# The last gather of each expert cut from 128 rows to 32, and its transpositions with it

## The chip, the cores and the metric

The kernel runs on one core of a Trainium2 chip. The metric is the device time of one execution in microseconds, the median of several runs. The engines are TensorE (PE, with its weight loads listed apart as PEld), VectorE (DVE), ScalarE (ACT), GpSimd (POOL) and SyncE (SP); sixteen DMA engines move data between HBM and SBUF.

## The reference, cut to what matters

A causal attention with a decaying bias gives 2304 rows of 512 features (`x`). A router then deals the rows out to eight experts, 288 rows each, and every expert runs two matrix products on its own rows. A dense two-layer network follows.

```python
N, D, E, F = (2304, 512, 8, 1024)
cap = N // E                      # 288 rows for each expert
logits = x @ w_gate
order = np.argsort(-logits.flatten())
# greedy: a row goes to the best expert that still has room
for e in range(E):
    mask = assigned == e
    h = np.maximum(x[mask] @ w1[e], 0.0)
    out[mask] = h @ w2[e]
# then, on all 2304 rows
h = np.maximum(x @ w_in, 0.0)
return h * h @ w_out
```

## The kernel before, in words

The attention stage writes its 2304 rows to a DRAM tensor `xd`. The routing (`route_phases`) finds one expert after the other; for the expert of number `e` it leaves a tile `idxs[e]` of 128 x 3 row numbers. Column 0 holds the rows in places 0 to 127 of that expert, column 1 those in places 128 to 255, and column 2 those in places 256 to 287; the other 96 entries of column 2 are 0.

`gather(e, c)` (line 1090) has POOL issue one indirect DMA for column `c`: 128 rows of 2 KB of `xd` land in `XG[:, c, :]`, one row in each partition. Three gathers make up an expert. `XG` is one buffer, so an expert's gathers start only when the transpositions of the expert before have read it.

The first expert product wants the features in the partitions. `xt(e, d)` (line 1095) makes the `d`-th block of 128 features: three transpositions on TensorE (line 1102), one for each `c`, go side by side into one PSUM tile `p`, with `XG[:, c, 128d:128d+128]` as the weights and the identity `cn.ident` as the moving operand. ACT and DVE then read `p[:, :CAP]`, that is 288 columns, and split them into a high and a low part (lines 1106 and 1107). The last 96 of the 384 columns that the transpositions write are not read. For expert 0 `xt0(c)` (line 1109) does the transpositions by `c` first, four feature blocks in a row (line 1113), as soon as that gather has landed; between them stand routing steps and warming products (line 1389).

The order of blocks (`order`) is written out by hand: products with `w1` (kind 1), with `w2` (kind 2), and the dense network in chunks of experts (kinds 3 and 4). `need(e)` queues the gathers and the `xt` steps of an expert, and the main loop pops them between blocks at due times. So on TensorE the three transpositions of an `xt` stand between matrix products, mostly alone, sometimes two `xt` in a row. POOL's queue holds the gathers, the indirect stores of result rows (line 1299) and some subtractions.

Lines 308 and 311 (attention, probabilities by values) and line 338 (transpositions of attention rows) are not touched by the change, but their rows are used below. Line 308 has weights of 64 columns and writes 64 PSUM partitions; line 338 has a form with weights of 64 columns, too.

Of the kernel before, what the change touches and what calls it, by code (L numbers as in the profile page):

```python
# [34 lines left out]
def f32(ap):  # L35
    return ap.bitcast(FT)
# [496 lines left out]
CAP = 288  # L533
# [480 lines left out]
def experts(tc, cn, L, xd, w1, w2, win, wout, out):  # L1014
    nc = tc.nc
    V, S, G, T = nc.vector, nc.scalar, nc.gpsimd, nc.tensor
# [53 lines left out]
    eids, idxs = [], []  # L1070
# [16 lines left out]
    XG = fx.tile([128, 3, DM], FT, name="rows")  # L1087
    XT, P0 = {}, []

    def gather(e, c):  # L1090

        G.indirect_dma_start(out=XG[:, c, :], out_offset=None, in_=xd,
                             in_offset=bass.IndirectOffsetOnAxis(ap=idxs[e][:, c:c + 1], axis=0))

    def xt(e, d, spare=False):
        if d == 0:
            XT[e] = (wk.tile([128, 4, CAP], FR, name="xH", bufs=1), wk.tile([128, 4, CAP], FR, name="xL", bufs=1))
        if e:
            p = ps.tile([128, 512], FT, name="h", bufs=2) if spare and cn.held and d % 2 else rps.tile(
                [128, 512], FT, name="mi")  # L1100
            for c in range(3):
                T.transpose(p[:, 128 * c:128 * c + 128], XG[:, c, 128 * d:128 * d + 128], cn.ident)  # L1102
        else:
            p = P0[d]
        hi, lo = XT[e]
        S.activation(hi[:, d, :], p[:, :CAP], AF.Copy)
        V.tensor_tensor(lo[:, d, :], p[:, :CAP], f32(hi[:, d, :]), op=OP.subtract)

    def xt0(c):
        for k in range(4):  # L1110
            if c == 0:
                P0.append(ps.tile([128, 512], FT, name=f"acc{k}"))
            T.transpose(P0[k][:, 128 * c:128 * c + 128], XG[:, c, 128 * k:128 * k + 128], cn.ident)

    RAWS, W = {}, {}

# [234 lines left out]
    def need(e):  # L1351
        if lw[0] is None:
            xrows(99)
            late_stores(nc, cn, 0)
            cn.otp.__exit__(None, None, None)
            lw[0] = pool("m_lw", 2, side="right")
        while len(idxs) <= e:

            route_step()
        if e not in gathered:  # L1360
            gathered.add(e)
            if e and [e - 1, e] in CHUNKS:

                for c in range(3):
                    gather(e, c)
                soon.extend((xt, (e, d, True), 0) for d in range(4))
                return
            for c in range(3):
                if e >= GE:
                    gathers.append((e, c, at[0] + GD + GS * c))  # L1370
                else:
                    gather(e, c)
            for d in range(4):
                side.append((xt, (e, d), at[0] + (GD + 2 * GS if e >= GE else 0) + SD))

    def side_step():
        f, a, _ = side.popleft()
        while f is xt and gathers:
            gather(*gathers.popleft()[:2])
        f(*a)  # L1380
# [14 lines left out]
    for c in range(3):  # L1395
        for _ in range(RF[2 * c]):
            route_step()
        xt0(c)
        if c < 2:
            warm(WU[c + 1])  # L1400
        for _ in range(RF[2 * c + 1]):
            route_step()
# [14 lines left out]
    for n, blk in enumerate(order):  # L1417
# [10 lines left out]
        if blk[0] == 1:  # L1428
            while any(a[0] == blk[1] for f, a, _ in soon):
                xt(*soon.popleft()[1])  # L1430
            while any(f is xt and a[0] == blk[1] for f, a, _ in side):
                side_step()
# [16 lines left out]
        k, e, f = blk  # L1449
        if k > 2:  # L1450
            e = CHUNKS[e][-1]
# [67 lines left out]
```

## Time and profile before

| | |
|---|---|
| median of 3 runs | 907.24 us (907.17 to 908.33) |
| the profiled execution | 909.57 us, of which the span from the first to the last instruction is 907.7 us |
| TensorE busy | 865.0 us, 95% of the span |
| VectorE, ScalarE, GpSimd busy | 62%, 51%, 31% |
| moved by DMA | 96.10 MB |
| mean granted TensorE clock | 0.977 of full speed |

A matrix product's row gives its start and a modelled duration that includes its way through the array, so products that follow each other overlap in the rows; what a product costs the engine is read from start to start. `PE` and `PEld` rows of one instruction belong together: the load of the weights, then the product. A number in square brackets is idle time of the engine ahead of the instruction, with what ended it.

### The profile page before, as it was taken

The numbers are of one execution on the slowest core, as the hardware profiler recorded it, in microseconds if no ns is written. First come the engines' busy times: TensorE is split into PE (matmuls) and PEld (weight loads), VectorE is DVE, ScalarE is ACT, GpSimd is POOL, SyncE is SP. The second block draws the span as 40 slices with busy tenths as digits, with TensorE's granted clock in tenths as the row PEclk, the third lists the DMA queues.
The fourth block names the chain that finished last, engine by engine and source line by source line (L and its number), as shares of the span: only waits on it lengthen the run. The fifth ranks groups of instructions, "written<-read, shape, count | busy, mean of one in ns | idle before, by whom it ended". The sixth has DMA issues, their size and how long they took to land.

```text
span 907.7 us, 17252 instructions
## 1 busy us (share of the span) xinstructions
PE 865.0 (95%) x6168; PEld 735.7 (81%) x6168; DVE 564.0 (62%) x1557; ACT 463.1 (51%) x1061; POOL 278.2 (31%) x259
## 2 busy tenths in 40 slices
PE   5899999998799899999999999999999999999996
PEld 4677777777599787889997888999788999898885
DVE  7687878877786779747757457677433353432222
ACT  7687778776235666534533233454333454543332
POOL 2555555530113355524001000201000534513323
PEclk9999999997799899999999999999999999999999
DMA  6787887834555623106522001752000440230001
GB/s 158 192 203 197 224 235 192 216 93 135 174 145 148 196 82 105 59 2 209 152 59 70 1 1 38 215 152 62 24 1 1 142 126 1 82 94 0 1 1 47
DMA packets 77285, 96.10 MB, mean 106 GB/s; under 512 B 10480, under 2 KB 55536, under 8 KB 77200
## 3 DMA queue, kind: packets, MB, share of 16 engines
q1 hardware_dynamic: 71184, 79.64, 31.6%
q0 software_dynamic: 3360, 11.01, 3.7%
q10 hardware_dynamic: 2656, 4.36, 1.5%
q8 instruction: 48, 0.79, 0.4%
q14 instruction: 37, 0.30, 0.1%
HBM read 80.83 MB, written 9.44 MB: 99 GB/s over the span
## 4 chain that ended last, share of the span: by engine, by line
PE 70%; DVE 5%; DMA 3%; issue 2%; ACT 1%; POOL 1%; SPq 0%; DVEq 0%; POOLq 0%; ACTq 0%
PE h L1135 11%; PE h L1136 11%; PE h L1137 11%; PE acc L1183 7%; PE acc L1184 7%; PE acc L1185 7%; PE acc L1135 4%; PE acc L1137 3%; PE acc L1136 3%; PE mi L744 2%; DMA raw<-in_w 1%; PE mi L1102 1%; PE acc L44 1%; DVE junk L244 1%; PE pt L278 1%
## 5 line engine op out<-in xcount | busy, mean ns | idle before, releaser
L1245 ACT ACTIVATE s<-h 128x512 f32<-128x512 f32 (+1 forms) x80 | 44.4, 556 | 200.1 <-PE h L1137 173.7
L1249 DVE TENSOR_TENSOR s<-s 128x512 f32<-128x512 f32 (+1 forms) x80 | 51.1, 639 | 140.7 <-ACT sH L1248 140.6
L1135 PE MATMUL h<-yH,winH 128*128 128x512 f32 (+1 forms) x332 | 123.3, 371 | 0.0
L1136 PE MATMUL h<-yL,winH 128*128 128x512 f32 (+1 forms) x332 | 120.9, 364 | 0.0
L1137 PE MATMUL h<-yH,winL 128*128 128x512 f32 (+1 forms) x332 | 120.7, 363 | 0.0
L1183 PE MATMUL acc<-wH,sH 128*128 128x512 f32 x288 | 114.8, 399 | 0.0
L1059 ACT ACTIVATE wH<-raw 128x512 fp32r<-128x512 f32 x128 | 79.8, 628 | 67.0 <-DMA raw<-in_w 41.5
L1185 PE MATMUL acc<-wH,sL 128*128 128x512 f32 x288 | 112.5, 390 | 0.0
L1184 PE MATMUL acc<-wL,sH 128*128 128x512 f32 x288 | 112.4, 390 | 0.0
L1250 POOL TENSOR_TENSOR sL<-s,sH 128x512 fp32r<-128x512 f32 (+1 forms) x48 | 68.1, 1418 | 131.0 <-DVE s L1249 131.0
L1062 DVE TENSOR_TENSOR wL<-raw,wH 128x512 fp32r<-128x512 f32 x104 | 74.4, 718 | 46.7 <-ACT wH L1059 44.4
L256 ACT ACTIVATE e<-sc,nm 128x576 f32<-128x576 f32 (+2 forms) x144 | 80.2, 557 | 36.7 <-DVE junk L244 34.2
L244 DVE TENSOR_SCALAR_CACHE_REDUCE junk<-sc 128x576 bf16<-128x576 f32 (+2 forms) x144 | 75.6, 525 | 35.4 <-PE sc L224 26.1
L1135 PE MATMUL h<-xH,wH 128*128 128x288 f32 x256 | 79.2, 309 | 2.5 <-DVE hL L1213 1.9
L1135 PE MATMUL acc<-hH,wH 128*128 128x288 f32 x256 | 78.3, 306 | 1.7 <-ACT wH L1059 1.7
L1137 PE MATMUL h<-xH,wL 128*128 128x288 f32 x256 | 76.7, 300 | 0.8 <-POOL wL L1062 0.8
L1136 PE MATMUL h<-xL,wH 128*128 128x288 f32 x256 | 77.0, 301 | 0.1
L1137 PE MATMUL acc<-hH,wL 128*128 128x288 f32 x256 | 76.2, 298 | 0.3 <-DVE wL L1062 0.3
L1136 PE MATMUL acc<-hL,wH 128*128 128x288 f32 x256 | 76.0, 297 | 0.0
L1137 PEld LDWEIGHTS h<-yH,winL 128*128 128x128 f32 x332 | 62.7, 189 | 10.7
L1135 PEld LDWEIGHTS h<-yH,winH 128*128 128x128 f32 x332 | 62.8, 189 | 10.1
L1136 PEld LDWEIGHTS h<-yL,winH 128*128 128x128 f32 x332 | 62.9, 189 | 9.6
(236 smaller groups left out, 2028.2 us busy)
## 6 DMA issues: line engine op xcount, KB each, us to landing
raw<-in_w SPq DMA_DIRECT2D x128, 256.0 KB
k<-in_kT SPq DMA_DIRECT2D x30, 288.0 KB
q<-in_qT SPq DMA_DIRECT2D x30, 288.0 KB
r<-in_wout SPq DMA_DIRECT2D x16, 512.0 KB
r<-in_win SPq DMA_DIRECT2D x15, 512.0 KB
vb<-in_vm SPq DMA_DIRECT2D x16, 256.0 KB
Q<-Q SPq DMA_DIRECT2D x16, 144.0 KB
QB<-Q SPq DMA_DIRECT2D x14, 144.0 KB
```

What stands on the lines that cost most here:

```text
L244: nc.vector.tensor_scalar(o, v, -0.125, None, op0=OP.mult, op1=OP.min, accum_out=nm[:m])
L256: nc.scalar.activation(o, v, AF.Exp, bias=nm[:m], scale=0.125, accum_out=sums[b % 2][:m, i, hd % H:hd % H + 1] if i else both[b % 2][:, p: ...
L1059: S.activation(hi, src, AF.Copy)
L1062: (G if eng[1] == "G" else V).tensor_tensor(lo, src, f32(hi), op=OP.subtract)
L1135: T.matmul(o, wh, xh, start=first, stop=False)
L1136: T.matmul(o, wh, xl, start=False, stop=False)
L1137: T.matmul(o, wl, xh, start=False, stop=last)
L1183: T.matmul(o, hi[:, c0:c0 + 128], wh, start=f == 0, stop=False)
L1184: T.matmul(o, hi[:, c0:c0 + 128], wl, start=False, stop=False)
L1185: T.matmul(o, lo[:, c0:c0 + 128], wh, start=False, stop=f == NB2 - 1)
L1249: V.tensor_tensor(s, s, s, op=OP.mult)
L1250: (V if CHUNKS[c][0] in QUIET else G).tensor_tensor(lo, s, f32(hi), op=OP.subtract)
```

## The change

The gather of column `c` fetches `m = min(128, CAP - 128 * c)` rows, so 128, 128 and 32. The transpositions use the first `m` partitions of `XG`, the upper left `m` x `m` corner of the identity, and write `m` columns. Their weights are then 32 rows by 128 columns for `c = 2`, the moving operand 32 x 32.

```diff
     def gather(e, c):
 
-        G.indirect_dma_start(out=XG[:, c, :], out_offset=None, in_=xd,
-                             in_offset=bass.IndirectOffsetOnAxis(ap=idxs[e][:, c:c + 1], axis=0))
+        m = min(128, CAP - 128 * c)
+        G.indirect_dma_start(out=XG[:m, c, :], out_offset=None, in_=xd,
+                             in_offset=bass.IndirectOffsetOnAxis(ap=idxs[e][:m, c:c + 1], axis=0))
+
+    def flip(p, c, d):
+        m = min(128, CAP - 128 * c)
+        T.transpose(p[:, 128 * c:128 * c + m], XG[:m, c, 128 * d:128 * d + 128], cn.ident[:m, :m])
 
     def xt(e, d, spare=False):
...
             for c in range(3):
-                T.transpose(p[:, 128 * c:128 * c + 128], XG[:, c, 128 * d:128 * d + 128], cn.ident)
+                flip(p, c, d)
...
-            T.transpose(P0[k][:, 128 * c:128 * c + 128], XG[:, c, 128 * k:128 * k + 128], cn.ident)
+            flip(P0[k], c, k)
```

## Rows read from the trace of the kernel before

**Rows 1.** The page, part 4: shares of the chain that ended last, by engine.
```profile
PE 70%; DVE 5%; DMA 3%; issue 2%; ACT 1%; POOL 1%; SPq 0%; DVEq 0%; POOLq 0%; ACTq 0%
```

**Rows 2.** Windows: length, then busy time (and instructions) by engine, clock, DMA share, GB/s.
```profile
core 0: us, PE busy (x) PEld busy (x) DVE busy (x) ACT busy (x) POOL busy (x), PEclk, DMA share, GB/s
230.00:245.00 15.00, 12.77 (x102) 8.57 (x103) 11.57 (x42) 3.85 (x9) 3.15 (x3) 0.73 0.60 188
...
317.00:900.00 583.00, 580.95 (x3753) 506.73 (x3751) 318.12 (x740) 252.05 (x474) 146.65 (x140) 1.00 0.22 66
```

**Rows 3.** The tile `rows` (XG): count, duration min/median/max in ns, first and last start, shape.
```profile
L1102 PE MATMUL mi<-ident,rows x78: 270/272/308, 271.8 to 743.7; 128*128 128x128 f32 x78
L1092 POOL DMA_INDIRECT rows<-xd,idx x24: 945/987/1455, 232.5 to 729.2; - x24
...
L1113 PE MATMUL acc<-ident,rows x12: 272/273/328, 236.2 to 240.6; 128*128 128x128 f32 x12
...
L1102 PE MATMUL h<-ident,rows x6: 272/272/273, 589.1 to 591.6; 128*128 128x128 f32 x6
...
DMA to landing us min/median/max: 3.3/4.0/5.7
```

**Rows 4.** Timeline of PE, then of PEld, at the first `xt` pair of expert 1.
```profile
271.81 0.81 PE L1102 MATMUL mi<-ident,rows 128*128 128x128 f32 x6
272.38 0.38 PE L1135 MATMUL acc<-hH,wH 128*128 128x288 f32 x1
272.60 0.29 PE L1136 MATMUL acc<-hL,wH 128*128 128x288 f32 x1
...
272.36 0.19 PEld L1135 LDWEIGHTS acc<-hH,wH 128*128 128x128 f32 x1
```

**Rows 5.** Timeline of PE at the last `xt` of expert 7.
```profile
743.47 0.49 PE L1102 MATMUL mi<-ident,rows 128*128 128x128 f32 x3
743.71 0.36 PE L1135 MATMUL h<-yH,winH 128*128 128x256 f32 x1
```

**Rows 6.** Timeline of PE in the attention: transpositions with weights of 64 columns.
```profile
99.39 0.60 PE L338 MATMUL pt<-ident,oT 128*64 128x128 f32 x4
99.82 0.27 PE L278 MATMUL pt<-ident,e 128*128 128x128 f32 x1
```

**Rows 7.** Timeline of PE and PEld around products that write 64 partitions (L308).
```profile
200.87 0.27 PE L282 MATMUL pt<-ident,e 128*128 128x128 f32 x1
...
201.07 0.19 PEld L308 LDWEIGHTS av<-eT,vb 128*64 128x64 f32 x3 [0.17 <-issue]
...
201.28 0.45 PE L308 MATMUL av<-eT,vb 128*64 128x192 f32 x6
201.66 0.44 PE L278 MATMUL pt<-ident,e 128*128 128x128 f32 x2
```

**Rows 8.** Groups of PE by shape: busy us, mean ns, idle before.
```profile
L308 PE MATMUL av<-eT,vb 128*64 128x320 f32 x180 | 27.5, 441 | 0.0
...
L308 PE MATMUL av<-eT,vb 128*64 128x64 f32 x60 | 4.3, 220 | 0.0
```

**Rows 9.** Groups of PEld by shape, with 128 and with 68 rows of weights.
```profile
L221 PEld LDWEIGHTS sc<-K,Q 128*128 128x128 f32 x160 | 32.0, 200 | 10.9 <-DVE Q L173 8.3 <-ACT e L256 2.1
...
L222 PEld LDWEIGHTS sc<-K,Q 68*128 68x128 f32 x80 | 15.3, 191 | 0.0
```

**Rows 10.** Timeline of PE (last row PEld) at expert 0's second and third transpositions.
```profile
238.82 0.66 PE L1113 MATMUL acc<-ident,rows 128*128 128x128 f32 x4 [0.24 <-DMA rows<-xd,idx]
239.31 0.38 PE L1389 MATMUL h<-onesb 128*128 128x512 bf16 x1
239.53 0.65 PE L744 MATMUL mi<-oh,wide 128*128 128x8 bf16 x20
240.21 0.65 PE L1113 MATMUL acc<-ident,rows 128*128 128x128 f32 x4
241.04 0.40 PE L1135 MATMUL h<-xH,wH 128*128 128x288 f32 x1 [0.17 <-ACT xH L1106]
...
239.50 0.58 PEld L744 LDWEIGHTS <-wide 128*128 128x128 bf16 x20 [0.20 <-DVE wide L640]
```

## The prediction

> **What bounds the kernel now.** I read the chain of work that ended last first, then busy time by stretch, then the touched tile, then TensorE's timeline around it. The chain is 70% TensorE, and GpSimd has 1% of it, DMA 3% [rows 1]. The stretches show why: from 317 to 900 us TensorE is busy 580.95 of 583.00 us at full clock, while GpSimd has 146.65 us of work there and the DMA engines are used to 22% [rows 2]. Whatever lengthens or shortens the engine's stream there moves the end by the same amount; GpSimd and DMA time there is free. Only the short stretch where expert 0 starts (230 to 245 us) is not of this kind: clock 0.73, TensorE idle at times, waits on gathers.
>
> The tile view of the gathered rows gives the counts [rows 3]: 24 gathers; 78 + 6 transpositions of line 1102, so 84, of which every third one, 28, is a third-column transposition of experts 1 to 7; and 12 of line 1113, of which 4 are expert 0's. So 8 gathers and 32 transpositions change. In the timeline the 84 stand in 22 runs: six runs of two `xt` (the first is in [rows 4]) and sixteen of one (the last is in [rows 5]). Hence 6 of the 28 are followed by another transposition, and 22 by a matrix product.
>
> **The gathers.** One costs GpSimd about 1 us (median 987 ns) and lands 3.3 to 5.7 us after its issue [rows 3]. A third gather with a quarter of the rows may cost GpSimd anything between the same and a quarter, so 0 to 0.75 us each, 6 us in all, and moves 192 KB less. All of this lies beside TensorE's stream. The rows of line 1102 show no wait for a gather: TensorE goes from a product into them without a gap [rows 4, 5]. For expert 0 the second gather is waited for (0.24 us), but it is issued ahead of the third and is not changed. The third column's transpositions start at 240.21, right behind the 20 small products of line 744, which began at 239.53 and wait on routing, not on rows [rows 10]. An earlier landing of the third gather therefore opens nothing. I take 0 us; if it did speed up expert 0 after all, the whole stay at 240.21 could only move up to the end of those products, so less than 0.05 us.
>
> **What a transposition costs now.** Six of them start at 271.81 and the load behind them at 272.36, so with the first one's load ahead they go at about 0.11 us apiece [rows 4]; the four with weights of 64 columns go at (99.82 - 99.39) / 4 = 0.11 us, too [rows 6]. Half the weights, same pace: the moving operand of 128 columns sets it, not the load. A column of fp32 moves in (441 - 220) / (320 - 64) = 0.86 ns [rows 8], so 128 take 0.11 us and 32 take 0.03 us.
>
> What follows a transposition limits the saving. The load of a product of line 1135 starts at 272.36; the product is recorded 0.02 us later but lasts 0.38 us against 0.29 us, so it is held up by 0.09 us and truly starts 0.11 us after its load [rows 4]. That load can start only with the last transposition, so with a 32-column transposition ahead the wait of 0.11 us stays: nothing saved in 22 of 28 cases. With another transposition behind it the load takes about 0.06 us: in [rows 7] the two of line 278 take 0.44 us against 0.27 + 0.11 = 0.38 us, because their first load had no cover. So 0.05 us are saved in 6 cases, 0.3 us, and about 0.2 us at expert 0's four. If nothing else happened, the sum would be -0.5 us.
>
> **What 32 rows may do to the array.** The trace has no product with 64 rows or fewer, so its cost is bounded from the nearest rows. Line 308 has weights of 64 columns and asks for no place in the array. Around it TensorE stands still: the transposition of line 282 starts at 200.87 and would be done with its columns after 0.11 us, but the next load starts at 201.07, with idle time marked ahead of it [rows 7]; that is 0.09 us. On the way back the last product of line 308 starts at 201.28 + 0.45 - 0.22 = 201.51 (64 columns, 220 ns, [rows 8]), its columns take 0.055 us, and the next load starts at 201.66: 0.095 us. In both directions the first load is not covered, another 0.06 us, or 0.11 us for the load of a product. So a change between the full array and a part of it empties the array, and costs 0.15 to 0.20 us.
>
> Does a 32-row transposition count as a part? For it: line 308 gets its part by its size alone. Against it: the transpositions with 64 weight columns in [rows 6] follow and precede full ones with no gap at all, and the loads with 68 rows [rows 9] belong to the full array. The Trainium skill (TensorEngine Tiling (Array Packing), Key Properties) states that changing the tiling mode drains TensorE; the gaps of [rows 7] agree with it. The same page (Restrictions) takes column tiling, but not row tiling, away from fp32 transpositions; by that, [rows 6] tells nothing of a transposition with few rows. I take the case with the drain, at a little over even odds, because the only rows of the trace that are small enough to fit a part pay for it unless they are transpositions cut in columns.
>
> The cost, then, of one third transposition with the drain: 0.09 idle, 0.06 its own uncovered load, 0.03 its columns, 0.09 idle, and 0.06 or 0.11 for the next load, together 0.33 or 0.38; less the 0.11 us of before, 0.22 or 0.27 us. Six times 0.22 and twenty-two times 0.27 make 1.3 + 5.9 = 7.2 us. At expert 0 the four stand together, so there is one change in (0.15 us) ahead of the first, whose way through the array is 96 x 0.86 ns = 0.08 us shorter; the change back hides under the wait for the split (TensorE idles there until 241.04 [rows 10]). That is 0.07 us. The sum is 7.3 us. The cover that other edits might have is absent: TensorE has 2 us of idle time in all between 317 and 900 us, and only expert 1's four transpositions (1.0 us of the 7.2) lie ahead of that.
>
> Against the profiled execution's own 909.57 us (span 907.7 and 1.9 around it) this gives 916.9. That execution was 2.3 us above the median of the runs shown; the same 7.3 us on the median of 907.24 give 914.5, which is my figure. Bounds of this case: the idle gaps alone, with every load covered, are 2 x 0.09 + 0.03 - 0.11 = 0.10 us each, 2.8 us, so 910; every load uncovered at 0.11 us, 0.32 us each, 9 us, so 916.5.
>
> **The rivals.** First: no part of the array, the 32 rows run as the 68 do. Then the sum is the -0.5 us above, 906.7 us (906.2 to 907.2), no change that can be told. For it speak [rows 6] and [rows 9]. Where this comes out, the gathers are hidden and the transposition is bound by the loads around it; that is also the case in which the change does less than it says.
>
> Second, the other side: load and columns both shrink with the rows, so a third transposition costs 0.03 us instead of 0.11 and the load behind it gets no slower. That is 0.08 x 28 = 2.2 us and some 0.2 us at expert 0, 904.8 us, 0.27% faster; it needs the load of the next product to be covered by something, which it has not in [rows 4]. A load of 68 rows lasts 191 ns on average and one of 128 rows 200 ns [rows 9], so rows hardly matter. The Trainium skill (TensorE: Matmul & The Clock Gate, LDWEIGHTS) says the same of a 32 x 128 load; by it this rival falls.
>
> **How the numbers follow.** What a measurement of this kernel can tell from no change is about 0.2%, 1.8 us. Drain: 0.57, all of it slower. No part of the array: 0.36, within 0.2%. Shrinking loads: 0.07, faster. The likeliest is 914.5 with its own range of 910.0 to 916.5. The range over the cases reaches down to the lower end of the first rival and up to that bound, 906.2 to 916.5, and leaves out the second rival and what lies beyond the bounds.
>
> **What the profile after would show.** Drain: in each `xt`, the load of the third transposition starts about 0.20 us after the second transposition, with idle time marked ahead of it, and the following load some 0.12 us after the third; the busy time of line 1102 falls while TensorE's span grows. First rival: third transpositions at a shorter duration (272 - 80 = some 190 ns) with no gaps, and the product behind them held up by 0.09 us as now. In every case GpSimd's gathers come out equal or shorter, and no wait on them appears. Wrong would I be if the gap around 32 rows were of another size than that around 64 columns, or if the clock of the stretch before 245 us were granted otherwise, which no row here lets me price.

## The result, and the profile after

| | before | changed |
|---|---|---|
| median | 907.79 us (907.17 to 908.45) | 915.0 us (913.83 to 915.5) |
| ratio | 1 | 1.0083, 95% interval 1.0069 to 1.0098 |
| profiled execution: time, span | 909.57, 907.7 us | 915.5, 913.6 us |

The changed kernel is slower by 6.3 to 8.9 us; 7.3 were forecast, 914.5 against the 915.0 measured.

The page of the changed kernel, first the busy times (engine, us, share of the span, instructions), then the chain of work that ended last, by engine:

```profile
PE 871.2 (95%) x6168; PEld 735.7 (81%) x6168; DVE 566.6 (62%) x1557; ACT 463.7 (51%) x1061; POOL 278.4 (30%) x259
...
PE 82%; DVE 6%; DMA 6%; issue 2%; ACT 2%; POOL 1%; SPq 0%; DVEq 0%; POOLq 0%; ACTq 0%
```

TensorE still sets the end, and its share of the chain is larger than in [rows 1]. The stretch that answers to [rows 2], up to the end of the 3753 instructions counted there:

```profile
core 0: us, PE busy (x) PEld busy (x) DVE busy (x) ACT busy (x) POOL busy (x), PEclk, DMA share, GB/s
317.00:906.00 589.00, 586.99 (x3753) 507.77 (x3751) 320.71 (x741) 253.27 (x475) 146.95 (x140) 1.00 0.21 63
```

The same 3753 products and transpositions are busy for 586.99 us instead of 580.95, at the same full clock; each window ends less than 0.5 us behind the last of them. So the whole 6 us are recorded as busy: the end of a matmul is modelled, and time between a matmul and its next load in which TensorE stands still can lie inside it. Busy time cannot tell standing still from work; starts, and the idle time ahead of loads, can.

The tile of gathered rows (count, duration min/median/max in ns, first and last start, shapes), beside [rows 3]:

```profile
L1098 PEld LDWEIGHTS mi<-ident,rows x78: 132/138/143, 271.1 to 749.5; 128*128 128x128 f32 x52, 32*128 32x128 f32 x26
L1098 PE MATMUL mi<-ident,rows x78: 242/271/328, 271.2 to 749.6; 128*128 128x128 f32 x52, 32*128 32x32 f32 x26
L1093 POOL DMA_INDIRECT rows<-xd,idx x24: 875/982/1457, 231.7 to 734.1; - x24
...
DMA to landing us min/median/max: 2.4/3.5/5.5
```

The gathers became cheaper at their lower end (875 ns against 945, landing from 2.4 us instead of 3.3), and GpSimd's whole busy time did not fall (278.4 us). Line 1098 is the old line 1102; lines 1140 to 1142 are the old 1135 to 1137.

The timeline at the first two `xt` of expert 1 (start in us, length, engine, line, operation, count, and in brackets the idle time ahead of it), beside [rows 4]:

```profile
271.18 1.09 PE L1098 MATMUL mi<-ident,rows 128*128 128x128 f32 x6
272.21 0.40 PE L1140 MATMUL acc<-hH,wH 128*128 128x288 f32 x1
272.45 0.30 PE L1141 MATMUL acc<-hL,wH 128*128 128x288 f32 x1
...
271.05 0.27 PEld L1098 LDWEIGHTS mi<-ident,rows 128*128 128x128 f32 x2
271.49 0.37 PEld L1098 LDWEIGHTS mi<-ident,rows 32*128 32x128 f32 x3 [0.17 <-issue]
272.03 0.13 PEld L1098 LDWEIGHTS mi<-ident,rows 32*128 32x128 f32 x1 [0.17 <-issue]
272.21 0.19 PEld L1140 LDWEIGHTS acc<-hH,wH 128*128 128x128 f32 x1
```

Read it by starts. From the first transposition to the second product (L1141) it was 272.60 - 271.81 = 0.79 us; now it is 272.45 - 271.18 = 1.27 us. Two loads stand behind 0.17 us of idle time: those of the two 32-row transpositions. Nothing that another engine does ends these waits; they are marked "issue".

At the last `xt` of expert 7, first the changed kernel, then the one product of the kernel before that follows on [rows 5]:

```profile
749.24 0.55 PE L1098 MATMUL mi<-ident,rows 128*128 128x128 f32 x3
749.72 0.39 PE L1140 MATMUL h<-yH,winH 128*128 128x256 f32 x1
749.95 0.28 PE L1141 MATMUL h<-yL,winH 128*128 128x256 f32 x1
```
```profile
743.91 0.28 PE L1136 MATMUL h<-yL,winH 128*128 128x256 f32 x1
```

A run of one `xt` took 743.91 - 743.47 = 0.44 us and now takes 0.71, so 0.27 more. Measured in this way, the 22 runs of `xt` sum to 13.55 us before and 20.58 after: 7.03 us more, on average 0.26 for each of the sixteen runs of one (4.2) and 0.48 for each of the six runs of two (2.9).

The spans differ by 5.9 us, not by 7.03. The first `xt` of the changed kernel's profiled execution begins 0.63 us earlier (271.18 against 271.81); its first gather already went out 0.76 us earlier (231.75 against 232.51), so this is not of the change's making. Of the 0.95 us that the four transpositions of expert 1 cost, 0.3 vanish ahead of 317 us, where TensorE still has idle time (ahead of line 754 at 312 us it was 1.27 us and is 0.55); from there to the next `xt` at 379 us both kernels are level. 7.03 - 0.63 - 0.3 = 6.1, which leaves 0.2 us unassigned.

### The profile page after: what moved, and what is told of

Its sections match the earlier page's. It is cut to its first block, busy times and chain, and to the rows that moved or that the text cites. A ratio compares the mean times of both kernels' runs of the same rounds, so it can differ in the third digit from the quotient of the medians.

```text
span 913.6 us, 17252 instructions
## 1 busy us (share of the span) xinstructions
PE 871.2 (95%) x6168; PEld 735.7 (81%) x6168; DVE 566.6 (62%) x1557; ACT 463.7 (51%) x1061; POOL 278.4 (30%) x259
## 4 chain that ended last, share of the span: by engine, by line
PE 82%; DVE 6%; DMA 6%; issue 2%; ACT 2%; POOL 1%; SPq 0%; DVEq 0%; POOLq 0%; ACTq 0%
PE h L1140 11%; PE h L1141 11%; PE h L1142 11%; PE acc L1188 7%; PE acc L1190 7%; PE acc L1189 7%; PE pt L278 4%; PE acc L1140 4%; PE acc L1142 3%; PE acc L1141 3%; PE av L308 3%; PE mi L744 2%; PE sc L221 2%; PE sc L222 2%; DMA QB<-Q 2%
## 5 line engine op out<-in xcount | busy, mean ns | idle before, releaser
L1141 PE MATMUL h<-yL,winH 128*128 128x512 f32 (+1 forms) x332 | 120.7, 364 | 0.0
L1141 PE MATMUL h<-xL,wH 128*128 128x288 f32 x256 | 76.9, 300 | 0.1
L1141 PE MATMUL acc<-hL,wH 128*128 128x288 f32 x256 | 76.4, 298 | 0.0
L1141 PEld LDWEIGHTS h<-yL,winH 128*128 128x128 f32 x332 | 62.7, 189 | 9.6
```

The lines of the kernel that those rows point to most:

```text
L1141: T.matmul(o, wh, xl, start=False, stop=False)
```

## The experiments

In the diffs, - is the changed kernel. Sums over the 22 runs of `xt` are always from the start of the first transposition to the start of the second product behind the last one.

**The gather alone.** The third column of `XG` is set to zero once, so that full transpositions find defined rows.

```diff
+    G.memset(XG[:, 2, :], 0.0)
...
-        m = min(128, CAP - 128 * c)
-        T.transpose(p[:, 128 * c:128 * c + m], XG[:m, c, 128 * d:128 * d + 128], cn.ident[:m, :m])
+        T.transpose(p[:, 128 * c:128 * c + 128], XG[:, c, 128 * d:128 * d + 128], cn.ident)
```

> The gather alone: the third gather fetches 32 rows, the transpositions turn 128 rows as before (rows 32 to 127 of the third column of the buffer are set to 0 once, by GpSimd, before the first gather). Theory (a transposition of 32 rows works on a part of the array, and going there and back empties the array): nothing of that is here, so the time of before, 907.8 us, within 1 us. Rival (the smaller gather is late, or takes the DMA engines or GpSimd in a worse way): 915 us.

Measured: 908.14 us, ratio to the kernel before 0.9996 (0.9981 to 1.001). Timeline of TensorE at the first two `xt`:

```profile
268.91 0.81 PE L1098 MATMUL mi<-ident,rows 128*128 128x128 f32 x6
269.48 0.38 PE L1140 MATMUL acc<-hH,wH 128*128 128x288 f32 x1
269.70 0.30 PE L1141 MATMUL acc<-hL,wH 128*128 128x288 f32 x1
```

0.79 us again, and 13.55 us over the 22 runs, as before the change. In the measured time the smaller gather neither gains nor costs anything that can be told.

**The transposition alone.** The gather fetches 128 rows again.

```diff
-        m = min(128, CAP - 128 * c)
+        m = 128
         G.indirect_dma_start(out=XG[:m, c, :], out_offset=None, in_=xd,
```

> The transpositions alone: the third gather fetches 128 rows as before, its transpositions turn 32 rows. Theory: all of the cost is here, 915.0 us, 0.26 us in each run of one step and 0.48 us in each run of two. Rival (gather): 907.3 us.

Measured: 915.26 us, ratio 1.0082 (1.0062 to 1.0102), the whole of the changed kernel's loss. The 22 runs sum to 21.32 us. The first alone takes 2.00 us; the other 21 sum to 19.32, against 20.58 - 1.27 = 19.31 in the changed kernel. The timeline at the first one shows why:

```profile
267.39 0.38 PE L1098 MATMUL mi<-ident,rows 128*128 128x128 f32 x2
268.44 0.79 PE L1098 MATMUL mi<-ident,rows 32*128 32x32 f32 x4 [0.66 <-DMA rows<-xd,idx]
...
269.39 0.30 PE L1141 MATMUL acc<-hL,wH 128*128 128x288 f32 x1
```

Here TensorE waits 0.66 us for the third gather of expert 1, which fetches 128 rows again. In this execution the `xt` came at 267.39, 3.8 us earlier than in the changed kernel's.

**64 and 96 rows.** Two kernels; in each, the line shown is changed twice, in the gather and in `flip`.

```diff
-        m = min(128, CAP - 128 * c)
+        m = (128, 128, 64)[c]
```
```diff
-        m = min(128, CAP - 128 * c)
+        m = (128, 128, 96)[c]
```

> 64 rows in place of 32, in the gather and in the transposition. Theory (a part of the array): the same idle stretch on both sides, and 32 columns more to move at 0.86 ns, 0.03 us in each of 32 transpositions, so 0.8 to 0.9 us above the changed kernel, 915.9 us. Rival (only a quarter of the array is a part, half of it runs like the whole): 907.5 us.

> 96 rows in place of 32, in the gather and in the transposition. Theory (a part is 64 rows or fewer; the loads with 68 rows belonged to the whole array): no idle stretch, 32 columns fewer than 128 to move, which shows only where another transposition follows (6 times 0.03 us), so the time of before, 907.6 us. Rival (any transposition with fewer than 128 rows, or with a corner of the identity, is held up): 913 to 916 us.

Measured: 64 rows 917.35 us, ratio 1.009 (1.0062 to 1.0119); 96 rows 908.77 us, ratio 0.9997 (0.9976 to 1.0018). The second pair of `xt` of expert 1 with 64 rows, then two `xt` with 96 rows (a pair further on, whose neighbours are products at full clock):

```profile
276.08 1.16 PE L1098 MATMUL mi<-ident,rows 128*128 128x128 f32 x6
277.41 0.30 PE L1141 MATMUL acc<-hL,wH 128*128 128x288 f32 x1
...
276.39 0.40 PEld L1098 LDWEIGHTS mi<-ident,rows 64*128 64x128 f32 x3 [0.17 <-issue]
276.96 0.14 PEld L1098 LDWEIGHTS mi<-ident,rows 64*128 64x128 f32 x1 [0.17 <-issue]
```
```profile
435.72 0.77 PE L1098 MATMUL mi<-ident,rows 128*128 128x128 f32 x6
436.27 0.38 PE L1140 MATMUL acc<-hH,wH 128*128 128x288 f32 x1
436.48 0.29 PE L1141 MATMUL acc<-hL,wH 128*128 128x288 f32 x1
...
435.59 0.68 PEld L1098 LDWEIGHTS mi<-ident,rows 128*128 128x128 f32 x6
```

64 rows: the same two gaps of 0.17 us, 1.33 us for the pair, 21.39 us in all. That is 0.81 over 32 rows, or 0.029 us for each of 28 transpositions; 32 more columns at 0.86 ns are 0.028. So the gaps don't depend on the columns, which are simply added. 96 rows: six loads in one piece with no gap, 0.76 us for the pair, 14.1 us in all. That is 0.55 over before and lies in expert 1's two runs, 0.51 of it in the first (1.30 us), where the third gather, of 96 rows, is waited for with 0.31 us of idle time. The price does not grow with the rows: 32 and 64 rows pay it, 96 and 128 don't.

**Third columns side by side.** Every second `xt` begins with its third column, so that in a run of two the two 32-row transpositions stand together: six changes there and six back fewer.

```diff
-            for c in range(3):
+            for c in ((2, 0, 1) if d % 2 else (0, 1, 2)):
```

> The same 32-row transpositions, in another order: odd feature blocks begin with the third column, even ones end with it. Where two steps follow each other (6 runs), the two 32-row transpositions are neighbours and share one stay in the part of the array. Theory (the change of mode costs, not the transposition): these 6 runs fall from 0.48 to about 0.17 us over before each, and 8 of the 16 single ones from 0.26 to 0.24, together 2.0 us less than the changed kernel, 913 us; in the trace 22 stays in place of 28. Rival (each 32-row transposition is slow by itself): 915.0 us, unchanged.

Measured: 911.97 us, ratio 1.0052 (1.0032 to 1.0072), against 1.0083 about 2.8 us less than the changed kernel where 2.0 were expected; the intervals don't tell these apart. One pair of this kernel, and a pair of the changed kernel:

```profile
435.71 0.98 PE L1098 MATMUL mi<-ident,rows 128*128 128x128 f32 x6
...
436.66 0.29 PE L1141 MATMUL acc<-hL,wH 128*128 128x288 f32 x1
...
435.58 0.27 PEld L1098 LDWEIGHTS mi<-ident,rows 128*128 128x128 f32 x2
436.02 0.44 PEld L1098 LDWEIGHTS mi<-ident,rows 32*128 32x128 f32 x4 [0.17 <-issue]
```
```profile
436.23 1.09 PE L1098 MATMUL mi<-ident,rows 128*128 128x128 f32 x6
...
437.49 0.30 PE L1141 MATMUL acc<-hL,wH 128*128 128x288 f32 x1
```

Same six transpositions, one marked gap instead of two, 0.95 us instead of 1.26, so the six pairs come out as expected, 0.17 over before. Eight of the single runs now begin with the 32-row transposition, and the idle time ahead of it falls outside a sum that starts there. Counted from the start of the product ahead, the 22 runs take 20.7 us against 23.1 in the changed kernel and 16.1 before: 2.4 less, 1.9 from the pairs and 0.6 from these eight, 0.07 each where 0.02 were expected. What is paid for is the change between shapes, not the small transposition.

**The third column twice.** Each `xt` does its third transposition a second time, between the two full ones.

```diff
-            for c in range(3):
+            for c in (0, 2, 1, 2):
```

> Each step of experts 1 to 7 turns the 32 rows twice, second and fourth (order 0, 2, 1, 2), so there are 28 more 32-row transpositions, each with a stay of its own; the second writes the same result again. Theory: 0.09 idle, 0.06 load, 0.03 columns, 0.09 idle, 0.06 load, 0.33 us for each of the 28 more, 9.2 us above the changed kernel, 924 us. Rival (only the work of the transposition counts): 28 times 0.06 us, 916.7 us.

Measured: 923.57 us, ratio 1.0178 (1.0159 to 1.0197), about 8.6 us over the changed kernel, 0.31 for each of 28; the 22 runs sum to 29.8 us, 9.22 more than 20.58, 0.33 each. A pair:

```profile
442.78 1.75 PE L1098 MATMUL mi<-ident,rows 128*128 128x128 f32 x8
444.46 0.40 PE L1140 MATMUL acc<-hH,wH 128*128 128x288 f32 x1
444.69 0.30 PE L1141 MATMUL acc<-hL,wH 128*128 128x288 f32 x1
```

1.91 us instead of 1.27, for two extra transpositions of 32 columns, whose columns alone take 0.06 us.

**The third column between the full ones.** Order 0, 2, 1, so that each run ends in a full transposition. Profiled once; only its trace is read.

```diff
-            for c in range(3):
+            for c in (0, 2, 1):
```

> The order of the three transpositions is 0, 2, 1, so a full one always follows the one of 32 rows and covers the load of the product. Theory: 0.24 us over before for each of 28 in place of 0.26 for 22 of them, 0.5 us below the changed kernel, which only the trace can tell: the uncovered load behind the part is then that of a transposition, 0.06 us, in all 28.

Measured: 19.62 us over the 22 runs, 0.96 less than the changed kernel, where 0.5 were expected. The direction is right, the size was expected too small by a slip in the expectation, not in the prediction. Its 0.24 for each of 28 is the mean of a run of two (0.48 / 2), in which one of the two stands ahead of a product; with a transposition behind every one of them the prediction's 0.22 holds for all 28. Measured are (19.62 - 13.55) / 28 = 0.22.

**32 rows gathered, 68 rows turned.** The gather of the change stays, the rows behind it are zero, the transposition takes 68 rows in the middle place, so that the product's load has a full transposition ahead of it.

```diff
+    G.memset(XG[:, 2, :], 0.0)
...
-        m = min(128, CAP - 128 * c)
+        m = (128, 128, 68)[c]
...
-            for c in range(3):
+            for c in (0, 2, 1):
```

> A version meant to keep both savings: the third gather fetches 32 rows, its transposition turns 68 rows (rows 32 to 127 of the third column are set to 0 once by GpSimd), in the order 0, 2, 1. Theory (68 rows belong to the whole array, and a full transposition follows): no idle stretch, and 0.05 us less than before in each of 28, 1.4 us, 0.15% below before: 906.4 us where before is 907.8. Rival (any corner is held up): 913 us or more.

Measured: 906.7 us, ratio to the kernel before 0.999 (0.9975 to 1.0006): well ahead of the changed kernel, not to be told from the one before. A pair:

```profile
433.20 0.73 PE L1099 MATMUL mi<-ident,rows 128*128 128x128 f32 x6
...
433.90 0.29 PE L1142 MATMUL acc<-hL,wH 128*128 128x288 f32 x1
```

0.70 us instead of 0.79, and 12.44 us over the 22 runs, 1.1 less than before where 1.4 were expected. With four rows more than the 64 that pay, the trace even shows a gain from the smaller shape and the order together, 0.04 us for each of 28; in the measured time it cannot be told from nothing.

## Why the prediction was right, step by step

**The figure.** The medians differ by 7.2 us, the forecast by 7.3; that they meet so closely is partly luck. The interval of the difference runs from 6.3 to 8.9 us, the forecast started from 907.24 where 907.79 were measured, and 0.3 us at expert 1 and the terms of expert 0 below came out otherwise. The likeliest case held; the range of 906.2 to 916.5 takes in no change, too, so it could hardly have told the two apart. Its upper end is also 0.3 above its own sum, 907.24 + 9.0 = 916.2.

**The bound.** Right. TensorE's stream from 317 us on became 6 us longer and the span followed.

**The gathers at nothing.** Right in the measured time, by the first experiment: they became cheaper (875 against 945 ns at the least), and no wait for a third gather stands in the profiles of the changed kernel or of the gather alone. But the cover is thinner than I took it to be. In the profile before expert 0 waited some 0.2 us for its third gather (below). With 128 and with 96 rows, in the second and fourth experiments, expert 1's first `xt` waited 0.66 and 0.31 us for one, and with 64 rows, in the third, expert 0 waited 0.21. The gather alone at 0.9996 leaves room for no more than 0.2% of gain; whether the smaller gather saves such waits often enough to matter stays open.

**32 rows count as a part of the array.** Right; this was the step at little over even odds. The second experiment puts the whole loss on the transposition, the third, fourth and eighth show that its size decides (32 and 64 rows pay, 68, 96 and 128 don't), the fifth and sixth that each change of shape is what costs. The first rival, with no part of the array, asked for 906.7 us and falls with 915.26. One ground was weaker than the prediction took it to be: half the products of line 308 write to PSUM partitions 64 to 127, so their place is set by more than their size. That TensorE empties itself at such a change is read from the gaps; the inside of the engine is shown by no run. The Trainium skill (TensorEngine Tiling (Array Packing), Key Properties) says that changing the tiling mode drains TensorE. The trace agrees with 0.09 us of standing still on either side of the 32 rows.

**The second rival**, shrinking loads, falls too: the groups by shape of the changed kernel (busy us, mean ns, idle before) give

```profile
L1098 PEld LDWEIGHTS mi<-ident,rows 128*128 128x128 f32 x52 | 6.2, 140 | 1.0
L1098 PEld LDWEIGHTS mi<-ident,rows 32*128 32x128 f32 x26 | 3.5, 133 | 4.4 <-issue 4.4
```

A quarter of the rows saves 7 ns of 140. The idle time ahead of the 26 is 4.4 us, 0.17 each. That is the emptying, 0.09 us, and the part of the transposition ahead, 0.08 us, beside which a load of 128 rows would have run.

**The terms of the sum.** With six runs of two at 0.22 + 0.27 = 0.49 and sixteen of one at 0.27, the forecast was 7.2 us; measured were 0.48 and 0.26, 7.03 us. The prediction wanted the load of the third transposition 0.20 us after the second one's start. The second one of the changed kernel's first run is

```profile
271.29 0.27 PE L1098 MATMUL mi<-ident,rows 128*128 128x128 f32 x1
```

and the load starts at 271.49, so 0.20 us: 0.11 of columns and 0.09 of standing still. "The following load some 0.12 us after the third" was told from the start of the third one's columns; as recorded, from load to load, it is 272.21 - 272.03 = 0.18 us, which is the same 0.06 + 0.03 + 0.09.

**A sign that failed.** The busy time of line 1102 was to fall. Windows over the tile of gathered rows for experts 1 to 7, before and after (PE, PEld and POOL busy):

```profile
269.00:750.00 481.00, 13.01 (x84) 9.77 (x84) 19.31 (x18) 0.99 0.29 89
```
```profile
269.00:752.00 483.00, 15.73 (x84) 10.33 (x84) 18.86 (x18) 0.99 0.28 85
```

It rose by 2.7 us, out of 7.0 that the runs cost. The single rows became shorter (276 to 269 ns on average in the 78), but they overlap less.

**Expert 0.** Two readings were wrong here, both small. The prediction had the third column's transpositions wait on routing and not on rows. In the kernel before, the third gather was issued at 235.22 and landed 4.9 us later, between 240.1 and 240.2; the last product of line 744 had started by then:

```profile
240.01 0.17 PE L744 MATMUL mi<-oh,wide 128*128 128x8 bf16 x1
```

The transpositions followed at 240.21 [rows 10], 0.20 us behind it. In the changed kernel the gather landed 4.6 us after 234.47, ahead of that product:

```profile
239.58 0.17 PE L744 MATMUL mi<-oh,wide 128*128 128x8 bf16 x1
239.68 0.43 PE L1098 MATMUL acc<-ident,rows 32*128 32x32 f32 x4
240.42 0.40 PE L1140 MATMUL h<-xH,wH 128*128 128x288 f32 x1 [0.31 <-ACT xH L1111]
...
239.67 0.32 PEld L1098 LDWEIGHTS acc<-ident,rows 32*128 32x128 f32 x4
```

The gather alone shows the same place with nothing to wait for and full transpositions:

```profile
237.32 0.17 PE L744 MATMUL mi<-oh,wide 128*128 128x8 bf16 x1
237.32 0.42 PEld L1098 LDWEIGHTS acc<-ident,rows 128*128 128x128 f32 x4
238.15 0.40 PE L1140 MATMUL h<-xH,wH 128*128 128x288 f32 x1 [0.17 <-ACT xH L1111]
```

From that last product to the first product of expert 0 it is 1.03 us before, 0.84 in the changed kernel and 0.83 with the gather alone. So between these executions the smaller gather saved 0.20 us in this place, where the prediction allowed it less than 0.05. In the second experiment, with 128 rows gathered, it was 0.84 us, so no such wait stood there; whether any of it reaches the end is not shown. The 32 rows then add 0.01, where 0.07 were forecast: the load waits 0.09 us behind the last product of line 744, against none with full transpositions, and the shorter way through the array gives 0.08 back, as the prediction had it (96 x 0.86 ns). No bracket marks these 0.09 us because the idle time ahead of the load is 0.02 us; it is read from starts. The 0.06 us of an uncovered load, the rest of the forecast's change in, are not added here.

**The cover.** The prediction saw that expert 1's 1.0 us lie ahead of full occupation and still counted it whole; 0.3 us of it were hidden.

## What to carry to other kernels

Fewer rows are not by themselves a cheaper transposition. Look at what stands before and behind it: here 32 rows between instructions with 128 rows cost 0.26 us each and 64 rows 0.28, where 68 rows cost nothing, so a short block is turned at 68 rows or more, or the short ones are put side by side. And judge such an edit by starts in the timeline of the engine that sets the end: the changed line's products became shorter on average while everything behind them came later.

## What was not expected

**In a transposition, rows decide and weight columns do not.** The transpositions with weights of 64 columns in [rows 6] go on at 0.11 us with no gap; with 64 rows there are two gaps. The two look alike in a list of shapes. No run cuts the rows without the moving columns, 32 with 32 and 64 with 64. Few moving columns alone open no gap between the products of line 744, which have 8 of them behind weights of 128 rows and start 0.025 us apart; but those are bf16 and no transpositions.

**The clock between 210 and 320 us differs between executions.** Windows of the kernel before, then of the gather alone:

```profile
210.00:320.00 110.00, 94.18 (x877) 85.50 (x876) 81.58 (x259) 53.87 (x140) 24.12 (x19) 0.84 0.54 167
```
```profile
210.00:320.00 110.00, 93.38 (x887) 84.00 (x888) 82.83 (x257) 55.30 (x137) 26.45 (x21) 0.91 0.54 164
```

The granted clock is 0.84 against 0.91: some 34 us of this stretch at 1.2 GHz against 20, the rest at 2.4. The spans are 907.7 and 905.0 us although the runs of `xt` take 13.55 us in both; the first `xt` already begins 2.9 us earlier (268.91 against 271.81), so the whole difference arises ahead of it. Single executions of the kernel before lay between 906.51 and 911.83 us beside the first four experiments. That is why one profiled span says nothing about an effect of 1 us here, and the sums over the runs do.
